# Seven products of halves for three experts: sums kept in PSUM, sums of weights and tokens placed by a table, a new order of all engines

## The chip, the cores and the metric

The kernel runs on one core of one Trainium2 chip. The metric is device time in microseconds (us), from runs of the whole kernel. The core has five engines that work side by side, each through its own queue in order: TensorE (PE in the rows, PEld for its weight loads), VectorE (DVE), ScalarE (ACT), GpSimd (POOL) and SyncE (SP), which here only issues transfers.

## The reference

Three layers follow one another. An mLSTM attention over 2 batches, 8 heads and 768 steps gives 1,536 tokens of 320 numbers. A dense layer with a rational function between its two products (320 to 2,048 to 320) follows. The last layer has four experts, whose outputs are added with a weight for each token:

```
def _moe2_ref(x, domain_probs, w1, w2):          # x (1536, 320), w1 (4, 320, 1024), w2 (4, 1024, 320)
    p = domain_probs / (domain_probs.sum(-1, keepdims=True) + 1e-09)
    out = np.zeros((N, D))
    for e in range(E):
        h = np.maximum(x @ w1[e], 0.0)
        out += p[:, e:e + 1] * (h @ w2[e])
    return out
```

The change is in experts 1 to 3 of this last layer, and in the order of the instructions from the dense layer on.

## The kernel before

**Numbers in two parts.** Every operand of a large product is held as a high part (fp32r) and a low part, the rest of the fp32 number. A product of a block is made of hi x hi, hi x lo, lo x hi, and for the last 64 of the 320 input rows (the "remainder") one matmul whose partitions hold these combinations side by side, 32 rows each.

**Seven products.** Experts 1 to 3 compute `x @ w1[e]` by Strassen's scheme in Winograd's form. The 320 inputs are cut in two (two blocks of 128 rows and a remainder of 2 x 32), the outputs of a block of 256 hidden units in two, and the tokens in two. A *stage* is one expert, one half `p` of the tokens (768) and one block `k` of 256 hidden units: 3 x 2 x 4 = 24 stages. A stage makes seven products of four matmuls of 384 columns (`product`, L1076), in three PSUM banks `ba`, `bb`, `bc` that come from a pool of two (`bank_new`), so that `bc` follows `ba` in its bank, the next stage's `ba` follows `bb`, and the next stage's `bb` follows `bc`. Products into a bank go on while VectorE takes partial sums out of it: `u2 = bb + s1` (L1154), `u3 = bb + s1` (L1162), `c21 = bb + s1` (L1173) and `c12 = bc + u2` (L1182), with `s1` a ScalarE copy of `ba`. `c22` is made by a ScalarE copy `s5` of `bc` (L1166) and a GpSimd sum `u3 + s5` (L1168). For each of the four blocks of the result ScalarE writes the relu as a high part (`relu`, L1096) and VectorE the low part (`low`, L1101). `low` reads `c` and the high part; for `c11` that is the bank `ba`, for `c21`, `c22`, `c12` a buffer in SBUF.

**Fills.** The second product (`g @ w2`) of a stage is 36 matmuls of 320 columns, which are laid between the products of the next stage, five or six at a time (`fill`, L1138). After the fourth `k` of a half, VectorE adds the six finished tiles to the output (`evac_exp`, L880), one in each fill.

**Preparation.** `prep(e, k)` loads a block of weights (9 transfers on SP), makes the sums of blocks that the scheme needs (4 of the main rows and 4 of the remainder, L1015) on GpSimd, lets ScalarE write the high parts (L1018, L1019, L1021), and subtracts for the low parts: main rows and second-layer weights on GpSimd (L1022, L1024), remainder rows on VectorE (L1023). `xprep(p)` does the like for a half of the tokens: sums on GpSimd and VectorE (L1040, L1046, L1057; L1057 writes three copies of each remainder half by three sums), low parts on both (L1050, L1064). Weights of expert 1 with `k` 0 and 1 and the tokens of half 0 go where the dense layer's weights were, those with `k` 2 and 3 where expert 0's weights are. The weights of the next expert are prepared during the four stages of the second half of the expert before. All temporary tiles come from five staging buffers (`stage`, L991).

**Order.** `ORDER` (L22) gives each engine a fixed order of its instructions, by their number in the order in which the program makes them. In the PE table, 2488 is the first matmul of stage 0; all before it in number belongs to earlier layers and expert 0. On VectorE the Strassen part begins with number 491, on ScalarE with 481, on GpSimd with 222, on SP with 95.

Of the kernel before, what the change touches and what calls it, by code (L numbers as in the profile page):

```python
# [92 lines left out]
    286-288 292-294 281 289 295 290 296-297 299 291 298 301-305 308 300 306 309-311 307 312-319 321-324 320 325-332  # L93
    334-338 343-344 333 345-348 340 339 349-350 341 351 342 352-357 361-362 358 363 359-360 364-366 368-370 367
    371-380 383-385 381 386-387 389 382 390 388 391-393 395-396 394 397-398 401 399 402 400 403-406 408-409 407 414
    410 415 411-412 416-417 413 418-423 425-429 424 430-434 436-441 435 442-445 448-449 447 450-453 446 454-458
    460-463 459 464 466-471 465 472-475 477-478 476 479-481 491 482 492 483 493 485 484 494 486 495-497 487 499-500
    488 498 501-503 489 504 490 519-521 505 522-527 506 528 507 529-533 508 534-535 509-510 536-537 511 513 538 514
    512 539-541 515 542-543 516-518 544-563 571 564-570 572-573 580 574-579 581-582 589 583-588 590-591 604 592-603
    605-643 651 644-650 652-653 660 654-659 661-662 669 663-668 670-671 684 672-683 685-754  # L100
# [15 lines left out]
    440-442 437 443 445-447 438 448-449 463 444 464 452-454 450 455 451 456 481-483 457 484-485 458 465-469 486 471  # L116
    470 487 472 474-475 488 473 490-491 476 489 492-494 477 495 478-480 511 496 512 497-498 513 499 514-517 500-501
    518-521 502 522-523 503 524-525 505-506 504 526-527 507-508 528-529 509-510 530-538 546 539 547 540-545 555-556
    549-550 548 551-554 564-565 558-559 557 560-563 573-574 567-568 566 569-572 575-598 606 599 607 600-605 615-616
    609-610 608 611-614 624-625 618-619 617 620-623 633-634 627-628 626 629-632 635-678  # L120
# [6 lines left out]
    133 143 132 150 144 148 153 149 151-152 136 145-146 154 157-158 155-156 160 159 167 222 161 223-225 162 226 228  # L127
    227 229 232 234 233 164 163 235-236 238 237 239 165-166 170 168-169 172 171 175 174 173 178 176-177 181 179-180
    182-188 190 189 191-192 194 193 195-196 198 197 200 199 202 201 204 203 206 205 208 207 210 209 212 211 214 213
    216 215 218 217 220 219 230 221 231 240 242 241 243-245 248 246 249 247 250-253 255 254 256-259 261 260 262 265  # L130
    267 266 269 268 270 263 288 264 271-273 275 274 276 289 277-278 281 279 282 280 283 290 284-286 294 287 295-298
# [1114 lines left out]
```

## Time and profile before

| | us |
|---|---|
| median of 3 runs | 689.5 (688.64 to 691.54) |
| the profiled execution, its own time | 691.14 |
| its span, first to last instruction | 689.3 |
| mean granted clock of TensorE | 0.97 of full speed |

| engine | busy us | share of the span |
|---|---|---|
| PE (matmul) | 623.3 | 90% |
| DVE | 497.0 | 72% |
| ACT | 370.5 | 54% |
| POOL | 372.0 | 54% |

The busy times are of the profiled execution. Busy time of PE contains matmuls that run at half clock, so a share of 90% is not the share of useful work.

### The profile page before, as it was taken

To read this page: it belongs to the slowest core of one execution; us is meant where nothing else is said; L and a number is where in the kernel's file an instruction comes from. 1 tells how busy PE (TensorE), PEld (TensorE's weight loads), DVE (VectorE), ACT (ScalarE), POOL (GpSimd) and SP (SyncE) were. 2 spreads that over 40 slices of the span, in tenths; PEclk is the share of its full clock that TensorE was granted. 3 is DMA by queue.
4 is the path that set the end of the run, shared out by engine and by line. 5 is a ranking of instruction groups with operands and counts; after the bars stand their busy time and mean duration, and the time that the engine had idled before them with its cause. 6 is when DMAs were issued, how large, how long until landed. Compare 5 with 4: busy or idle time off the path is not lost.

```text
span 689.3 us, 11395 instructions
## 1 busy us (share of the span) xinstructions
PE 623.3 (90%) x4300; PEld 601.9 (87%) x4300; DVE 497.0 (72%) x755; ACT 370.5 (54%) x682; POOL 372.0 (54%) x395
## 2 busy tenths in 40 slices
PE   3898999999999999999998866889869988899997
PEld 1888999999999999999997766889769988899997
DVE  8889999999887686676777678865764456643544
ACT  5989977576667557686873523334422244332221
POOL 6678897567774434353479867725841037421010
PEclk9889999999999999999999978999999999999999
DMA  7884431202200000000000200211210012000101
GB/s 209 256 250 134 123 118 57 84 24 77 88 20 0 2 0 1 1 2 1 2 20 11 63 19 16 57 36 48 56 48 1 1 34 54 24 1 0 58 1 58
DMA packets 21383, 35.46 MB, mean 51 GB/s; under 512 B 3377, under 2 KB 14129, under 8 KB 21329
## 3 DMA queue, kind: packets, MB, share of 16 engines
q1 hardware_dynamic: 21328, 34.74, 17.2%
q8 instruction: 34, 0.56, 0.4%
q14 instruction: 21, 0.16, 0.1%
...
## 4 chain that ended last, share of the span: by engine, by line
PE 55%; DVE 25%; ACT 6%; issue 5%; POOL 5%; DMA 2%; SPq 0%; ACTq 0%; POOLq 0%; DVEq 0%
PE h L1080 14%; PE acc L1114 14%; PE h L756 13%; PE acc L768 12%; DVE ar L1023 3%; DVE fb L637 2%; DVE ar L1101 2%; DMA so<-in_o_gate_dram 1%; DVE h L794 1%; DVE cv_t L379 1%; DMA qkt<-in_qk_dram 1%; ACT ar L1096 1%; DVE so L880 1%; POOL stg_r L1015 1%; POOL ar L1022 1%
## 5 line engine op out<-in xcount | busy, mean ns | idle before, releaser
L1080 PE MATMUL h<-ar,ar 128*128 128x384 f32 (+1 forms) x408 | 103.9, 353 | 29.4 <-DVE u L1154 13.0
L768 PE MATMUL acc<-wout,g 128*128 128x320 f32 x576 | 127.6, 320 | 1.7 <-POOL g L258 0.6
L756 PE MATMUL h<-x,win 128*128 128x256 f32 x768 | 126.5, 288 | 1.4 <-DVE s__2895 L795 0.7
L756 PEld LDWEIGHTS h<-x,win 128*128 128x128 f32 x768 | 107.8, 190 | 3.4 <-issue 0.9
L1080 PEld LDWEIGHTS h<-ar,ar 128*128 128x128 f32 (+1 forms) x408 | 73.2, 196 | 34.4 <-DVE u L1154 15.0
L1168 POOL TENSOR_TENSOR c<-u,s 128x384 f32<-128x384 f32 x24 | 24.3, 1013 | 134.6 <-ACT s L1166 134.6
L768 PEld LDWEIGHTS acc<-wout,g 128*128 128x128 f32 x576 | 93.1, 189 | 4.0 <-POOL g L258 1.1
L1114 PE MATMUL acc<-ar 128*128 128x320 f32 x432 | 81.8, 319 | 0.0
L1114 PE MATMUL acc<-ar,ar 128*128 128x320 f32 x432 | 80.0, 313 | 0.0
L1101 DVE SCALAR_TENSOR_TENSOR ar<-c,ar 128x384 fp32r<-128x384 f32 x72 | 57.6, 827 | 29.5 <-ACT ar L1096 29.4
L1096 ACT ACTIVATE ar<-c 128x384 fp32r<-128x384 f32 x72 | 35.9, 520 | 74.5 <-DVE c L1182 39.0
L1114 PEld LDWEIGHTS acc<-ar 128*128 128x128 f32 x432 | 73.0, 197 | 0.0
L756 PE MATMUL h<-x,we 128*128 128x256 f32 x384 | 71.4, 286 | 0.8 <-DVE g L805 0.8
L1114 PEld LDWEIGHTS acc<-ar,ar 128*128 128x128 f32 x432 | 71.1, 192 | 0.0
L768 PE MATMUL acc<-we,g 128*128 128x320 f32 x288 | 59.4, 320 | 4.9 <-ACT g L804 2.7
L756 PEld LDWEIGHTS h<-x,we 128*128 128x128 f32 x384 | 58.4, 192 | 1.6 <-DVE g L805 1.3
L1080 PE MATMUL h<-x,ar 128*128 128x384 f32 x216 | 51.4, 347 | 6.5 <-DVE c L1173 6.5
L1166 ACT ACTIVATE s<-h 128x384 f32<-128x384 f32 x24 | 11.8, 491 | 77.7 <-PE h L1080 77.7
L768 PEld LDWEIGHTS acc<-we,g 128*128 128x128 f32 x288 | 45.8, 193 | 6.9 <-ACT g L804 3.5
L1080 PEld LDWEIGHTS h<-x,ar 128*128 128x128 f32 x216 | 37.9, 195 | 7.2 <-DVE c L1173 6.8
L1173 DVE TENSOR_TENSOR c<-h,s 128x384 f32<-128x384 f32 x24 | 13.3, 556 | 38.3 <-PE h L1080 38.2
L1015 POOL TENSOR_TENSOR stg_m<-stg_m 128x128 f32<-128x128 f32 x48 | 28.4, 607 | 13.4 <-DMA stg_m<-in_moe_w_dram 13.4
...
## 6 DMA issues: line engine op xcount, KB each, us to landing
...
```

Of the source, the lines that this page charges most:

```text
L637: V.tensor_tensor_scan(W, src, id4f, 0.0, op0=ALU.mult, op1=ALU.add)
L756: PE.matmul(o, w5[:, j, fs], r, start=(n == 0), stop=(n == len(seq) - 1))
L768: PE.matmul(acc[t], x, y, start=(first and a == 0 and n == 0), stop=(last and a == nff - 1 and n == 2))
L1015: G.tensor_tensor(out=b[:, d], in0=b[:, x], in1=b[:, y], op=op)
L1023: V.tensor_tensor(out=wr[KR:2 * KR], in0=r7[KR:2 * KR], in1=wr[KR:2 * KR].bitcast(F32), op=ALU.subtract)
L1080: PE.matmul(bank, w, x, start=(first and n == 0), stop=(n == 3), skip_group_check=True)
L1096: A.activation(g[:, 0], c, AF.Relu)
L1101: V.scalar_tensor_tensor(out=g[:, 1], in0=c, scalar=0.0, in1=g[:, 0].bitcast(F32), op0=ALU.max, op1=ALU.subtract)
L1114: PE.matmul(acc[t], g[:, x, w * P:(w + 1) * P], wo[:, y, a], start=(k == 0 and a == 0 and n == 0), stop=(k == NK - 1 and a == 1 and n == 2))
L1166: A.activation(s5, bc, AF.Copy)
L1168: G.tensor_tensor(out=c22, in0=u3, in1=s5, op=ALU.add)
L1173: V.tensor_tensor(out=c21, in0=bb, in1=s1, op=ALU.add)
```

## The change

Four things change. **In the stage:** `c22` becomes one VectorE sum of the bank `bc` and `u3`, ScalarE applies the relu in place and writes the high part by a second instruction, and GpSimd writes the low part; `s5` goes. `c21` and `c12` are written back into their banks instead of into SBUF, and `relu` and `low` read them there. **In the preparation:** each sum and each low part goes to the engine that a string `ws` names. In the order in which it is read: `prep(1,0)` and `prep(1,1)` (11 instructions each) on VectorE, the 17 of `xprep(0)` on VectorE, `prep(1,2)` and `prep(1,3)` on GpSimd, of `xprep(1)` 15 on VectorE and its two main low parts on GpSimd, and all eight preparations for experts 2 and 3 on GpSimd. **In the remainder of the tokens:** one sum of 64 partitions is made, six SP transfers copy its halves to three places each, and seven copies with seven low parts become four and four. **In the order:** the tables are new from there to the end. The PE table lays numbers 2488 to 2502, the first 15 matmuls of stage 0, between the last matmuls of expert 0. The VectorE table swaps each `evac_exp` with the sum that follows it.

In the new numbering VectorE's Strassen part runs from 491: `prep(1,0)` 491-501, `prep(1,1)` 502-512, `xprep(0)` 513-529, `xprep(1)` 530-544, then 8 for each stage (`u2`, low of `c11`, `u3`, `c22`, `c21`, low of `c21`, `c12`, low of `c12`) and 6 more in each stage with `evac_exp`; stage 0 is 545-552, stage 4 is 577-590, stage 8 is 615-628. On GpSimd 222-243 are `prep(1,2)` and `prep(1,3)`, 244-245 the two of `xprep(1)`, then comes one low part of `c22` for each stage (246 for stage 0), and from stage 5 on the preparations. On ScalarE a stage is six numbers (505-510 for stage 0), and 540-542 is `prep(2,0)`. On SP the transfers of `xprep(0)` are 113-118 and those of `xprep(1)` 137-142.

```
--- before.py
+++ after.py
+    2298-2301 2305 2302-2304 2306-2316 2318-2335 2348-2351 2488-2489 2336-2337 2342-2343 2352-2353 2338-2341
+    2344-2347 2354-2363 2376-2382 2490 2492 2364-2365 2370-2371 2383-2384 2493-2494 2366-2369 2372-2375 2385-2391
+    2404-2410 2392-2393 2398-2399 2411-2412 2394-2397 2400-2403 2413-2419 2432-2438 2491 2420-2421 2426-2427
+    2439-2440 2496 2422-2425 2428-2431 2441-2447 2460-2466 2495 2448-2449 2454-2455 2467-2468 2450-2453 2456-2459
+    2469-2475 2497-2501 2476-2477 2482-2483 2502 2478-2481 2484-2487 2503-4023
...
+    472-475 477-478 476 479-481 499-501 482 510-511 513 483 512 514-516 485 484 517 519 518 521 520 486 522 487
+    523-524 526 525 527-528 488 529 489 545 490 546-549 551 550 552-560 530-531 561 532-533 562 534 563-564 535-536
+    565-568 537 569 541 538-539 570-571 540 542 572-576 543-544 578 577 580 579 582 581 584 583 586 585 587 589 588
+    590-614 616 615 618 617 620 619 622 621 624 623 625 627 626 628-652 654 653 656 655 658 657 660 659 662 661 663
...
+    467-469 471 470 487-488 472 474-475 473 489-492 476 505 477-478 506 479-480 493-494 507 509 508 510 495 511
+    496-497 512 498 513-518 499 519-520 500 521-523 501-502 524 503-504 525-533 540 534 541 535-539 549 543 542 544
...
+    201 204 203 206 205 208 207 210 209 212 211 214 213 216 215 218 217 220 219 221-222 224 223 225-226 228 227 229
+    233 235 234 236-237 239 238 240 230 246 231-232 241-242 247 243-244 248 245 252 254 253 255 249 256 258 257 259
+    264 266 265 267-268 270 269 271 250 260-261 276 251 277-279 272 262 273 263 280 282 281 284 274 283 288 290 289
+    285 291-292 275 293-296 286 297 304 306 305 307 287 308 310 309 316 311 317 298 318-320 299 321-323 300-302
...
+    103 93 95-96 106-109 97-102 104-105 110-162 169 163-168 170-180 187 181-186 188-198 205 199-204 206-207 214
+    208-213 215-226
...
+    ws="VVVVVVVVVVVVVVVVVVVVVVVVVVVVVVVVVVVVVVVGGGGGGGGGGGGGGGGGGGGGGVVVVVVGGVVVVVVVVVGGGGGGGGGGGGGGGGGGGGGGGGGGGGGGGGGGGGGGGGGGGGGGGGGGGGGGGGGGGGGGGGGGGGGGGGGGGGGGGGGGGGGGGG",
...
-            tr = [t[:, n] for n in range(7)]
+            tr = {B11: t[:, 0:1], B21: t[:, 1:3], T1: t[:, 3:5], T2: t[:, 5:7]}
         else:
             t = ar[1][0:96, o + 8 * HT:o + 11 * HT].rearrange("p (n t) -> p n t", n=3)
-            tr = [t[:, n] for n in range(3)]
-            for n in range(2):
-                t = g_p.tile([P, 1024], F32R, tag="g", name="xr")[0:96, 0:2 * HT].rearrange("p (n t) -> p n t", n=2)
-                tr += [t[:, 0], t[:, 1]]
+            tr = {B11: t[:, 0:1], B21: t[:, 1:3]}
+            for n in (T1, T2):
+                tr[n] = g_p.tile([P, 1024], F32R, tag="g", name="xr")[0:96, 0:2 * HT].rearrange("p (n t) -> p n t", n=2)
         xv.append((tm, tr))
...
-                    G.tensor_tensor(out=b[:, d], in0=b[:, x], in1=b[:, y], op=op)
+                    tt("ws", b[:, d], b[:, x], b[:, y], op)
...
-            G.tensor_tensor(out=wm[:, 1], in0=m7, in1=wm[:, 0].bitcast(F32), op=ALU.subtract)
-            V.tensor_tensor(out=wr[KR:2 * KR], in0=r7[KR:2 * KR], in1=wr[KR:2 * KR].bitcast(F32), op=ALU.subtract)
-            G.tensor_tensor(out=wo[:, 1], in0=w3, in1=wo[:, 0].bitcast(F32), op=ALU.subtract)
+            tt("ws", wm[:, 1], m7, wm[:, 0].bitcast(F32), ALU.subtract)
+            tt("ws", wr[KR:2 * KR], r7[KR:2 * KR], wr[KR:2 * KR].bitcast(F32), ALU.subtract)
+            tt("ws", wo[:, 1], w3, wo[:, 0].bitcast(F32), ALU.subtract)
...
-        def sums(r, np_, eng):
+        def sums(r, np_):
...
-                eng.tensor_tensor(out=o, in0=x0, in1=x1, op=op)
+                tt("ws", o, x0, x1, op)
             return ta, tb
 
         def main():
             r = [stage("xm")[:, 0:2 * HT] for j in range(2)]
-            for j, e in ((0, G), (1, V)):
-                e.tensor_tensor(out=r[j], in0=xj[0][j].bitcast(F32), in1=xj[1][j].bitcast(F32), op=ALU.add)
-            for n, t in enumerate(sums(r, P, G)):
+            for j in range(2):
+                tt("ws", r[j], xj[0][j].bitcast(F32), xj[1][j].bitcast(F32), ALU.add)
+            for n, t in enumerate(sums(r, P)):
                 hi, lo = tm[:, 0, 2 * n:2 * n + 2], tm[:, 1, 2 * n:2 * n + 2]
                 A.activation(hi, t, AF.Copy)
-                (V, G)[n].tensor_tensor(out=lo, in0=t, in1=hi.bitcast(F32), op=ALU.subtract)
+                tt("ws", lo, t, hi.bitcast(F32), ALU.subtract)
 
         def rem():
+            o = stage("xo")[:, 0:2 * HT]
+            tt("ws", o, xj[0][2].bitcast(F32), xj[1][2].bitcast(F32), ALU.add)
             r = [stage("xe")[0:96, 0:2 * HT] for j in range(2)]
             for j in range(2):
-                k = slice(j * KR, (j + 1) * KR)
                 for q in range(3):
-                    (G, V)[j].tensor_tensor(out=r[j][q * KR:(q + 1) * KR], in0=xj[0][2][k].bitcast(F32),
-                                            in1=xj[1][2][k].bitcast(F32), op=ALU.add)
-            ta, tb = sums(r, 96, G)
+                    SY.dma_start(out=r[j][q * KR:(q + 1) * KR], in_=o[j * KR:(j + 1) * KR])
+            ta, tb = sums(r, 96)
             r0, r1 = [t.rearrange("p (b t) -> p b t", b=2) for t in r]
-            for n, t in ((B11, r0[:, 0]), (B21, r1[:, 0]), (B22, r1[:, 1]), (T1, ta[:, 0]), (T3, ta[:, 1]),
-                         (T2, tb[:, 0]), (T4, tb[:, 1])):
-                A.activation(tr[n], t, AF.Copy)
-                V.tensor_tensor(out=tr[n][2 * KR:3 * KR], in0=t[2 * KR:3 * KR], in1=tr[n][2 * KR:3 * KR].bitcast(F32),
-                                op=ALU.subtract)
+            for n, t in ((B11, r0[:, 0:1]), (B21, r1), (T1, ta), (T2, tb)):
+                d = tr[n]
+                A.activation(d, t, AF.Copy)
+                tt("ws", d[2 * KR:3 * KR], t[2 * KR:3 * KR], d[2 * KR:3 * KR].bitcast(F32), ALU.subtract)
         return main, rem
 
...
-        return h, l, tr[n]
+        m = max(k for k in tr if k <= n)
+        return h, l, tr[m][:, n - m]
...
+        c22 = el_new("r", 2, "c22")
+        V.tensor_tensor(out=c22, in0=bc, in1=u3, op=ALU.add)
+        A.activation(c22, c22, AF.Relu)
+        g22 = g_new(1)
+        A.activation(g22[:, 0], c22, AF.Copy)
+        G.tensor_tensor(out=g22[:, 1], in0=c22, in1=g22[:, 0].bitcast(F32), op=ALU.subtract)
         product(bb, k, A22, p, T4, False)
-        s5 = el_new("x", 3, "s5")
-        A.activation(s5, bc, AF.Copy)
-        c22 = el_new("r", 2, "c22")
-        G.tensor_tensor(out=c22, in0=u3, in1=s5, op=ALU.add)
-        r22 = relu(c22, 1)
         fill(5)
         product(bc, k, S4, p, B22, False)
-        c21 = el_new("y", 4, "c21")
-        V.tensor_tensor(out=c21, in0=bb, in1=s1, op=ALU.add)
-        r21 = relu(c21, 0)
+        V.tensor_tensor(out=bb, in0=bb, in1=s1, op=ALU.add)
+        r21 = relu(bb, 0)
         g21 = low(r21)
-        g22 = low(r22)
         fill(6)
         q = (n - 1) % len(stages)
         if n and stages[q][1] == 1 and stages[q][0] < NE - 1:
             pre[stages[q][0] + 1, stages[q][2]][1]()
-        c12 = el_new("r", 2, "c12")
-        V.tensor_tensor(out=c12, in0=bc, in1=u2, op=ALU.add)
-        g12 = low(relu(c12, 1))
+        V.tensor_tensor(out=bc, in0=bc, in1=u2, op=ALU.add)
+        g12 = low(relu(bc, 1))
```

## Rows read from the trace of the kernel before

**Rows 1.** Windows from 350 us to PE's end: us, busy time by engine, PEclk, DMA.

```profile
350.00:390.20 40.20, 35.43 (x241) 33.56 (x240) 29.09 (x28) 19.10 (x35) 35.46 (x27) 0.96 0.13 37
390.20:447.10 56.90, 42.61 (x222) 39.98 (x221) 45.12 (x44) 20.79 (x40) 41.73 (x41) 0.85 0.11 30
447.10:523.30 76.20, 64.08 (x386) 62.64 (x385) 48.87 (x65) 26.73 (x48) 39.84 (x51) 0.98 0.15 42
523.30:553.90 30.60, 30.60 (x195) 30.60 (x194) 14.46 (x28) 9.14 (x19) 3.09 (x4) 1.00 0.00 1
553.90:606.95 53.05, 44.84 (x257) 43.79 (x256) 32.90 (x42) 19.36 (x35) 26.40 (x27) 0.94 0.14 37
606.95:685.50 78.55, 77.24 (x486) 76.45 (x484) 37.76 (x72) 21.36 (x45) 8.75 (x8) 1.00 0.06 21
```

**Rows 2.** Waits of PE from 380 us: us in total, times, longest.

```profile
PE h L1080 <- DVE u L1154: 13.0, 7, 3.0
PE h L1080 <- DVE c L1182: 12.3, 7, 3.2
PE h L1080 <- DVE c L1173: 6.5, 1, 6.5
```

**Rows 3.** Timeline of POOL, 393.7 to 402.2 us: start, us, line, shapes.

```profile
393.75 2.12 POOL L1022 TENSOR_TENSOR ar<-stg_m,ar 128x896 fp32r<-128x896 f32 x1
...
399.11 2.06 POOL L1022 TENSOR_TENSOR ar<-stg_m,ar 128x896 fp32r<-128x896 f32 x1
```

**Rows 4.** Timeline of DVE in the same stretch.

```profile
394.20 7.92 DVE L1023 TENSOR_TENSOR ar<-stg_r,ar 32x896 fp32r<-32x896 f32 x1
```

**Rows 5.** Instructions of L1101 (whole span) and L1023 (280 to 450 us): ns min/median/max.

```profile
L1101 DVE SCALAR_TENSOR_TENSOR ar<-c,ar x72: 545/559/3159, 403.3 to 681.3; 128x384 fp32r<-128x384 f32 x72
L1101 DVE SCALAR_TENSOR_TENSOR ar<-h,ar x24: 547/557/558, 393.2 to 674.2; 128x384 fp32r<-128x384 f32 x24
...
L1023 DVE TENSOR_TENSOR ar<-stg_r,ar x4: 1080/1712/7917, 353.6 to 407.8; 32x896 fp32r<-32x896 f32 x4
```

**Rows 6.** Groups of DVE and POOL, 447.1 to 685.5 us: busy us, mean ns.

```profile
L1023 DVE TENSOR_TENSOR ar<-stg_r,ar 32x896 fp32r<-32x896 f32 x8 | 17.4, 2177 | 0.2
...
L1168 POOL TENSOR_TENSOR c<-u,s 128x384 f32<-128x384 f32 x20 | 20.3, 1015 | 126.6 <-ACT s L1166 126.6
L1022 POOL TENSOR_TENSOR ar<-stg_m,ar 128x896 fp32r<-128x896 f32 x8 | 17.4, 2170 | 6.7 <-ACT ar L1018 6.7
L1015 POOL TENSOR_TENSOR stg_m<-stg_m 128x128 f32<-128x128 f32 x25 | 16.0, 651 | 11.6 <-DMA stg_m<-in_moe_w_dram 11.6
L1015 POOL TENSOR_TENSOR stg_r<-stg_r 96x128 f32<-96x128 f32 x28 | 13.7, 507 | 4.6 <-DMA stg_r<-in_moe_w_dram 4.4
L1024 POOL TENSOR_TENSOR ar<-stg_w,ar 128x640 fp32r<-128x640 f32 x8 | 12.8, 1600 | 3.5 <-ACT ar L1021 3.1 <-PE h L1080 0.4
```

**Rows 7.** Timeline of PE over the end of one undisturbed stage.

```profile
637.52 1.04 PE L1114 MATMUL acc<-ar 128*128 128x320 f32 x6
638.40 0.69 PE L1080 MATMUL h<-x,ar 128*128 128x384 f32 x3
...
639.84 0.69 PE L1080 MATMUL h<-ar,ar 128*128 128x384 f32 x3
```

**Rows 8.** Timeline of DVE in the same stage.

```profile
636.29 0.56 DVE L1173 TENSOR_TENSOR c<-h,s 128x384 f32<-128x384 f32 x1 [2.31 <-PE h L1080]
637.55 1.03 DVE L1101 SCALAR_TENSOR_TENSOR ar<-c,ar 128x384 fp32r<-128x384 f32 x2 [0.71 <-ACT ar L1096]
```

**Rows 9.** Timeline of ACT in the same stage.

```profile
639.16 0.53 ACT L1096 ACTIVATE ar<-c 128x384 fp32r<-128x384 f32 x1 [1.65 <-DVE c L1182]
```

**Rows 10.** Timeline of DVE near 345 us: L794 writes PSUM, L795 SBUF.

```profile
344.55 0.69 DVE L794 SCALAR_TENSOR_TENSOR h<-s__4022,h 128x512 f32<-128x512 f32 x1
345.27 0.69 DVE L795 SCALAR_TENSOR_TENSOR s__4022<-h,r__4024 128x512 f32<-128x512 f32 x1
```

**Rows 11.** Transfers that SP issues at the end: ns min/median/max.

```profile
L882 SPq DMA_DIRECT2D out_dram<-so x6: 332/332/345, 682.4 to 686.1; - x6
```

More of the change, by code (lines that the diff above doesn't have):

```diff
@@ L92 @@
     267-268 237 269 234 270-271 224-225 272 275-276 273 277 274 235 278 239 279 240 280 246-248 282-285 249 238
[L93 to L100, printed above, removed]
+    286-288 292-294 281 289 295 290 296-297 299 291 298 301-305 308 300 306 309-311 491 307 492-494 312-316 495
+    317-319 321-324 320 325-332 334-338 343-344 333 496-497 345-348 340 339 349-350 341 498 502 351 342 352-354
+    503-504 355-357 361-362 358 363 359-360 364-366 505-506 508 507 509 368-370 367 371-380 383-385 381 386-387 389
+    382 390 388 391-393 395-396 394 397-398 401 399 402 400 403-406 408-409 407 414 410 415 411-412 416-417 413
+    418-423 425-429 424 430-434 436-441 435 442-445 448-449 447 450-453 446 454-458 460-463 459 464 466-471 465
+    472-475 477-478 476 479-481 499-501 482 510-511 513 483 512 514-516 485 484 517 519 518 521 520 486 522 487
+    523-524 526 525 527-528 488 529 489 545 490 546-549 551 550 552-560 530-531 561 532-533 562 534 563-564 535-536
+    565-568 537 569 541 538-539 570-571 540 542 572-576 543-544 578 577 580 579 582 581 584 583 586 585 587 589 588
+    590-614 616 615 618 617 620 619 622 621 624 623 625 627 626 628-652 654 653 656 655 658 657 660 659 662 661 663
+    665 664 666-690 692 691 694 693 696 695 698 697 700 699 701 703 702 704-728 730 729 732 731 734 733 736 735 738
+    737 739 741 740 742-772
     """,
@@ L115 @@
     399 409-410 405 416-417 413 418 411 414 419 415 420 422-424 412 425-427 421 428-429 432-434 430 435-436 439 431
[L116 to L120, printed above, removed]
+    440-442 437 443 445-447 438 448-449 463 444 464 452-454 450 455 451 456 481-483 457 484-485 458 465-466 486
+    467-469 471 470 487-488 472 474-475 473 489-492 476 505 477-478 506 479-480 493-494 507 509 508 510 495 511
+    496-497 512 498 513-518 499 519-520 500 521-523 501-502 524 503-504 525-533 540 534 541 535-539 549 543 542 544
+    550 545-548 558 552 551 553-554 559 555-557 567 561 560 562 568 563-566 570 569 571-593 600 594 601 595-599 609
+    603 602 604 610 605-608 618 612 611 613-614 619 615-617 627 621 620 622-623 628 624-626 630 629 631-672
     """,
@@ L126 @@
     82 125 124 81 86 122 129 101 87-88 126-127 134 89 130 128 102-103 94 137 131 104 140 135 138 142 139 147 117 141
[L127 to L131, printed above, removed]
[L132 to L135 removed]
+    133 143 132 150 144 148 153 149 151-152 136 145-146 154 157-158 155-156 160 159 167 161-162 164 163 165-166 170
+    168-169 172 171 175 174 173 178 176-177 181 179-180 182-188 190 189 191-192 194 193 195-196 198 197 200 199 202
+    201 204 203 206 205 208 207 210 209 212 211 214 213 216 215 218 217 220 219 221-222 224 223 225-226 228 227 229
+    233 235 234 236-237 239 238 240 230 246 231-232 241-242 247 243-244 248 245 252 254 253 255 249 256 258 257 259
+    264 266 265 267-268 270 269 271 250 260-261 276 251 277-279 272 262 273 263 280 282 281 284 274 283 288 290 289
+    285 291-292 275 293-296 286 297 304 306 305 307 287 308 310 309 316 311 317 298 318-320 299 321-323 300-302
+    312-313 328 303 329-331 324 314 325 315 332 334 333 336 326 335 340 342 341 337 343 327 344 346 345 348 338 347
+    349 339 350-357
     """,
```

9 lines of the change are left out of this document (removed).

## Prediction

> **What bounds the kernel now.** I read the page first (PE 90% busy, DVE and POOL far less), then windows from 350 us on, then the waits of PE, then the timelines of DVE and POOL around the longest waits. The windows show where time is lost [rows 1]. From 523.3 to 553.9 us three stages take 30.60 us and PE is busy all of it: a stage without a wait is 10.2 us. Its 36 fills take 0.147 us each (six between 637.52 and 638.40 [rows 7]), 5.3 us together, so the 28 matmuls of the products are 4.9 us. Against this measure:
>
> - 390.2 to 447.1, stages 0 to 3: 56.9 us; stage 0 has no fills, so 4.9 + 3 x 10.2 = 35.5 are needed: 21.4 lost.
> - 447.1 to 523.3, stages 4 to 9: 76.2 - 61.2 = 15.0 lost.
> - 523.3 to 553.9: nothing.
> - 553.9 to 606.95, stages 13 to 16: 53.05 - 40.8 = 12.25 lost.
> - 606.95 to 685.5, stages 17 to 23 and the last 36 fills: 78.55 - 71.4 - 5.3 = 1.85 lost.
> - 350 to 390.2, the end of expert 0: 40.2 - 35.43 = 4.8 idle, and a granted clock of 0.96 for another 1.6: 6.4 lost.
>
> That is 50.5 us in the stages and 6.4 ahead of them; idle time is not all of it, since at clocks of 0.85 and 0.94 matmuls after a wait run partly at the lower level. Every large wait of PE is for DVE: `u2`, `c12`, `c21` [rows 2]. These sums are short; what is late is the DVE queue ahead of them. At 394.20 one subtraction of the weights (L1023) took 7.92 us [rows 4], where four such took 1.08 at least [rows 5]. It ended 0.95 us after a run of POOL instructions that lasted from 393.75 to 399.11 + 2.06 = 401.17 [rows 3]. The eight later ones took 2.18 on average [rows 6]. `low` shows which operands matter: from a bank (`h`) it took 547 to 558 ns in 24 cases, from SBUF 545 to 3159 in 72 [rows 5]. So a DVE instruction whose two tensors both lie in SBUF waits for POOL; one with an operand in PSUM does not. The chain is PE, behind DVE, behind POOL.
>
> The Trainium skill (SBUF — State Buffer, section "Who interferes with whom") states the same split, one SBUF input against two, and adds that the loser waits for the whole instruction of the other. The 7.92 us of the trace are longer than any one POOL instruction, so here the measurement goes further than the page. By the page alone the wait at 394.20 would have ended with the POOL instruction then running, at 393.75 + 2.12, some 5 us sooner; by the page, then, rival 1 below has no such form, and the trace of this kernel shows that it has.
>
> **Stages 5 to 23.** Before, a stage has eight DVE instructions, three of which read SBUF twice (low of `c21`, `c22`, `c12`), and L1023 comes once for each of eight preparations. After, it has eight as well: `c22` comes, its low part goes to POOL, and all others have one operand in PSUM. L1023 goes to POOL. So no DVE instruction of these stages meets POOL any more, and of the 15.0 + 12.25 + 1.85 = 29.1 us (nothing in stage 4) nearly all should go. A write into PSUM costs DVE no more: 0.69 beside 0.69 [rows 10]. ScalarE gives up `s5` and gains a copy: one for one.
>
> Two things are new. First, POOL. A preparation cost it 4 x 0.65 + 4 x 0.51 + 2.17 + 1.60 = 8.4 us, and a stage 1.0 for `c22` [rows 6]. Now L1023 is added; POOL's price for 32 partitions is not shown, and lies between DVE's 1.08 [rows 5] and the 2.17 of 128 partitions; I take 2.2, since 96 partitions of L1015 cost nearly as much as 128. The low part of `c22` costs the 1.0 of the sum it replaces. That is 11.6 us for a stage of 10.2 in four stages running: 5.6 us late at their end. Weights of `k` are free after stage `k` of the second half and wanted four stages later, some 30 us of room, and `g22` is first read at the 22nd of the next stage's 36 fills. POOL stays off the path; if this room were gone, each expert would wait 5.6.
>
> Second, the banks are held longer. The next stage's `ba` waits for the low part of `c21`, its `bb` for that of `c12`, where before both waited only for the sum. In the undisturbed stage `c21` begins at 636.29 and takes 0.56, the relu 0.53 [rows 9], the low part 0.56: with three hand-overs of 0.05 to 0.1 it is done by 638.1, and `ba` is wanted at 638.40 [rows 7, 8]. For `c12` the relu also waits until the fills have read the buffer that it overwrites, at 637.52 + 1.04 = 638.56; then 0.53 + 0.56 and three hand-overs, 639.8 to 639.95, where `bb` is wanted at 639.84. So this chain just fits, or is 0.1 us late in each stage: 19 x 0.05 = 1. The ScalarE table lays a high part of weights ahead of this relu (540 ahead of 534), in the time in which the relu waits anyway; I add 1 us for eight such stages. The swaps with `evac_exp` take away the 0.6 that these cost before.
>
> With 1 more for what I don't see, 3 of 29.1 are left: **-26**. Ends: all goes (-29), or the bank chain is 0.5 late in 19 stages, 9.5, and 3 stay (-17).
>
> **Stages 0 to 4.** 15 of the 28 matmuls of stage 0 now run ahead of it (2.6 us of work). Weights `k` 0 and 1 and tokens 0 are done on DVE ahead of stage 0; `k` 2 and 3 on POOL in stages 0 and 1, 2 x (2.2 + 2.2 + 1.6) = 12 us, which ends about when stage 2 wants them. What stays is `xprep(1)`: 15 DVE instructions that read SBUF twice, spread by the table over the end of stage 1 to the beginning of stage 4 (530 to 544), while POOL works on `k` 3 and on sums for expert 2. Uncontended, by 1.08 us for 896 columns [rows 5], some 14 x 0.6 to 1.0 = 11 us in three stages, where DVE has 8 x 0.56 = 4.5 of its own in 10.2: it fits. With POOL each can wait 0.5 (a sum) to 2.1 (a low part); I take 0.7 on average, 10 us, of which half falls into DVE's free time. So I expect 5 us of waits, 2 of lower clock behind them, and 3 at the start of stage 0, where no fills cover the sums: 10.5 left of 21.4, **-11**. The last two low parts (543, 544) come behind the low part of `c12` of stage 3, and stage 4's second product needs the last of them at once: 1.5 to 3 of the 5. Ends: 4.5 left (-17); as much lost as before (0).
>
> The six transfers for each half are issued by SP at 0.33 each [rows 11], 2 us, and loads are queued behind them. For tokens 0, two sums with the results of expert 0 behind them wait on DVE until they have landed; an estimate from the last output (issued at 686.1, over at the span's end, 689.3) is 3 us each. The table puts other work between; if this cover fails, it costs 3 us.
>
> **Ahead of stage 0.** The 15 matmuls and a DVE without POOL beside it fill about half of the 6.4 lost: **-3** (0 to -5). The 16 sums of weights that move to DVE earlier, in the dense layer, cost it some 0.3 each by the same 1.08, and POOL is relieved of as many: 0, plus or minus 1.5.
>
> **Sum.** -26 - 11 - 3 = -40 from 691.14, the profiled execution's own time, gives 651. The median of the runs is 1.6 below that execution; I take 650 for the median after.
>
> **Rivals.**
> 1. *DVE starves at the front.* If `xprep(1)` meets POOL as L1023 did at 394.20, one such case costs 7, and stages 0 to 4 lose the 21 of before: 650 + 11 = 661. For it: 15 instructions, and POOL busy there. Against: POOL's runs are then of shorter instructions for the most part, 0.5 to 0.65 for a sum [rows 6].
> 2. *The bank chain is the new bound.* At 0.5 us late in each of 23 stages: 650 + 11 = 661. For it: no slack at 639.84. Against: the hand-overs in the rows are under 0.1.
> 3. *POOL falls behind* with the weights of experts 2 and 3, at stages 8 and 16: 2 x 8 = 16, so 666. It needs POOL at 1.7 times its rows: 4 x (19.7 - 10.2) = 38, 8 more than the room of 30.
> 4. *Waits only move*: the same loss in other places, 690.
> 5. *Slower:* the bank chain again, with the relu of `c12` stuck behind other ScalarE work (high parts of weights, copies). It decides from 40 / 23 = 1.75 us a stage; at 2.2 it would give 700. Such work would have to come first in each stage, and only eight stages have high parts of weights.
>
> **How the numbers follow.** My forecast, 640 to 660, has 0.58; rival 1 0.18; rival 2 0.14; rival 3 0.04; rival 4 0.03; rival 5 0.03. The range runs from 638 (all ends good but a little) to 667 (rivals 1 to 3 in). 0.5%, 3.4 us, is about what a measurement can tell from no change: faster 0.94, same 0.03, slower 0.03.
>
> **What would show it.** Right: `low` at 0.55 us throughout, PE without waits from stage 5 on and stages of 10.2 to 10.3 us, PE's waits all in stages 0 to 4, clock 1.00 after. Wrong: waits of `product` for the low part in every stage (rival 2), DVE instructions of `xprep` over 2 us (rival 1), waits for POOL's low parts of weights (rival 3).

## The result, and the profile after

The median fell from 689.07 us (4 runs, 688.63 to 691.54) to 639.14 us (4 runs, 637.76 to 646.54): ratio 0.929, 95% interval 0.9216 to 0.9365. 650 was forecast, with a range of 638 to 667. The profiled executions are 691.14 and 639.66, so -51.5 is to be explained.

The head of the page of the kernel after: busy time, share and count of each engine, and the clock by slices.

```profile
PE 609.8 (96%) x4300; PEld 592.6 (93%) x4300; DVE 450.5 (71%) x773; ACT 372.2 (58%) x676; POOL 334.2 (52%) x361
...
PEclk9879999999999999999999999999999999999999
```

PE went from 90% to 96% of a shorter span, and the granted clock is at 0.9 or more from the fourth of the 40 slices on. The waits of PE from 380 us, the view of [rows 2]:

```profile
PE h L1084 <- DVE ar L1105: 1.2, 1, 1.2
PE h L1084 <- DVE xr L263: 1.1, 1, 1.1
PE acc L773 <- DVE g L810: 0.2, 1, 0.2
```

The long waits for `u2`, `c12` and `c21` are gone. Windows, the view of [rows 1], cut where PE ends a stage: from the end of expert 0, stages 0 to 4, 5 to 10, 11 to 13, 14 to 18, 19 to 23:

```profile
351.50:388.95 37.45, 35.72 (x254) 34.26 (x253) 27.93 (x38) 19.24 (x33) 10.21 (x18) 1.00 0.22 59
388.95:435.46 46.51, 44.20 (x270) 42.81 (x270) 32.16 (x57) 23.54 (x41) 26.90 (x29) 1.00 0.19 47
435.46:497.00 61.54, 61.54 (x388) 61.43 (x387) 29.70 (x55) 26.69 (x48) 43.20 (x51) 1.00 0.19 52
497.00:527.30 30.30, 30.30 (x192) 30.27 (x191) 15.98 (x30) 11.39 (x22) 8.71 (x9) 1.00 0.07 20
527.30:578.34 51.04, 51.04 (x321) 50.96 (x321) 24.76 (x46) 21.81 (x40) 29.24 (x28) 1.00 0.10 27
578.34:634.50 56.16, 56.16 (x357) 55.94 (x355) 27.97 (x52) 15.58 (x31) 5.08 (x5) 1.00 0.08 29
```

From stage 5 on elapsed time and PE's busy time are the same number in every row, although POOL is busier than before in the stages that prepare weights (43.20 of 61.54 in stages 5 to 10, against 39.84 of 76.20 in stages 4 to 9 [rows 1]). `low`, which took up to 3159 ns before [rows 5]:

```profile
L1105 DVE SCALAR_TENSOR_TENSOR ar<-h,ar x72: 539/557/560, 387.3 to 629.8; 128x384 fp32r<-128x384 f32 x72
```

### The profile page after: what moved, and what is told of

The parts are those of the page before. It is cut to its first block, busy times and chain, and to the rows that moved or that the text cites. A ratio compares the mean times of both kernels' runs of the same rounds, so it can differ in the third digit from the quotient of the medians.

```text
span 637.8 us, 11387 instructions
## 1 busy us (share of the span) xinstructions
PE 609.8 (96%) x4300; PEld 592.6 (93%) x4300; DVE 450.5 (71%) x773; ACT 372.2 (58%) x676; POOL 334.2 (52%) x361
## 4 chain that ended last, share of the span: by engine, by line
PE 69%; DVE 20%; ACT 6%; issue 2%; POOL 1%; DMA 1%; SPq 0%; ACTq 0%; POOLq 0%; DVEq 0%
PE acc L1118 19%; PE h L1084 17%; PE h L761 15%; PE acc L773 13%; DVE fb L642 2%; DVE ar L263 1%; DVE h L799 1%; PE sc L669 1%; DVE cv_t L384 1%; PE o L694 1%; DVE g L810 1%; DVE x L742 1%; DVE qc L650 1%; DVE fb L674 1%; PE dl L709 1%
## 5 line engine op out<-in xcount | busy, mean ns | idle before, releaser
L1084 PE MATMUL h<-ar,ar 128*128 128x384 f32 (+1 forms) x408 | 99.4, 338 | 0.0
L1118 PE MATMUL acc<-ar 128*128 128x320 f32 x432 | 78.6, 309 | 0.0
L1100 ACT ACTIVATE ar<-h 128x384 fp32r<-128x384 f32 x72 | 35.3, 491 | 73.7 <-PE h L1084 46.8
L1105 DVE SCALAR_TENSOR_TENSOR ar<-h,ar 128x384 fp32r<-128x384 f32 x72 | 40.0, 556 | 48.0 <-ACT ar L1100 47.1
L1173 POOL TENSOR_TENSOR ar<-c,ar 128x384 fp32r<-128x384 f32 x24 | 24.4, 1016 | 93.7 <-ACT ar L1172 88.8
L1084 PEld LDWEIGHTS h<-ar,ar 128*128 128x128 f32 (+1 forms) x408 | 70.4, 188 | 0.8 <-DVE u L1166 0.3
L1118 PEld LDWEIGHTS acc<-ar 128*128 128x128 f32 x432 | 69.6, 188 | 0.0
L1170 ACT ACTIVATE c<-c 128x384 f32<-128x384 f32 x24 | 12.6, 526 | 60.3 <-DVE c L1169 60.3
L263 POOL TENSOR_TENSOR stg_m<-stg_m 128x128 f32<-128x128 f32 x40 | 19.5, 507 | 40.1 <-DMA stg_m<-in_moe_w_dram 24.1
L1158 DVE TENSOR_TENSOR u<-h,s 128x384 f32<-128x384 f32 x24 | 13.3, 556 | 24.6 <-PE h L1084 24.6
```

Of the source, the lines that this page charges most:

```text
L263: return ENG[alt(kind)].tensor_tensor(out=out, in0=in0, in1=in1, op=op)
L1084: PE.matmul(bank, w, x, start=(first and n == 0), stop=(n == 3), skip_group_check=True)
L1100: A.activation(g[:, 0], c, AF.Relu)
L1105: V.scalar_tensor_tensor(out=g[:, 1], in0=c, scalar=0.0, in1=g[:, 0].bitcast(F32), op0=ALU.max, op1=ALU.subtract)
L1118: PE.matmul(acc[t], g[:, x, w * P:(w + 1) * P], wo[:, y, a], start=(k == 0 and a == 0 and n == 0), stop=(k == NK - 1 and a == 1 and n == 2))
L1158: V.tensor_tensor(out=u2, in0=bb, in1=s1, op=ALU.add)
```

## The experiments

Theory P is that of the prediction: a VectorE instruction with two operands in SBUF waits for GpSimd's reads, and TensorE waits behind VectorE. Theory Q is that the new tables and the different load of VectorE made the gain, theory B that sums in place hold the banks too long. The table gives, beside the medians, the distance between the starts of `u2` (read from VectorE's timeline) of stages 0 and 5, and of stages 5 and 23; at 10.18 a stage, 18 stages are 183.2. Two things are to be kept in mind. The `u2` of stage 0 runs among the last matmuls of expert 0 where 15 matmuls of stage 0 are moved there, so the column 0 to 5 of f1 can't be set against that of after. And in the kernel before the first wait of stage 5 lies ahead of its `u2`, so 2.6 us that stages 5 to 23 lose stand in the column 0 to 5.

| kernel | median us | u2 of 0 to 5 | u2 of 5 to 23 |
|---|---|---|---|
| before | 689.07 | 70.98 | 209.42 |
| b1, before, GpSimd only writes | 668.14 | 68.71 | 186.54 |
| b3, before, remainder low parts on GpSimd | 681.13 | 72.80 | 200.49 |
| b4, b3 and sums in place | 687.49 | 66.06 | 207.63 |
| after | 639.14 | 54.20 | 183.61 |
| a1, after, sums in SBUF | 648.63 | 58.39 | 189.10 |
| a2, after, remainder low parts on VectorE | 657.70 | 55.37 | 201.63 |
| a3, a1 and a2 | 668.90 | 59.43 | 207.97 |
| a4, after, c22 as before | 662.86 | 65.75 | 195.28 |
| f1, after, early matmuls moved back | 642.39 | 50.72 | 183.86 |
| f2, after, evac_exp not swapped | 647.17 | 55.84 | 190.08 |
| f4, after, GpSimd reads during xprep(1) | 644.20 | 58.89 | 183.91 |

Medians of the kernel before, in the groups of runs beside these: 690.74 (b3, b4, f4), 690.87 (a4, f1, f2), 691.50 (b1, a1 to a3). They lie 1.7 to 2.4 us above the 689.07 beside after, and after was not run again in these groups, so a difference of medians to 639.14 is uncertain by about as much. The traces allow a second count, from the start of the 2,529th matmul, which in all of these kernels is the same point ahead of stage 0 (350.2 us before, 351.6 after), to the end. By it a1, a2, a3, a4, f1, f2 and f4 are 9.4, 18.9, 29.3, 22.9, 3.6, 7.8 and 4.7 us longer than after, and b1, b3 and b4 are 25.5, 7.4 and 7.1 shorter than before.

**Do GpSimd's reads cause the loss?** b1 changes GpSimd alone:

```
-    G.tensor_tensor(out=b[:, d], in0=b[:, x], in1=b[:, y], op=op)
+    G.memset(b[:, d], 0.0)                     # experts 2 and 3; likewise for L1022 and L1024
```

> The kernel before, in which GpSimd's sums and low parts of the weights of experts 2 and 3 are replaced by fills with zero of the same tiles (same count and order on every engine, but GpSimd reads nothing there); the weights of experts 2 and 3 are therefore not the reference's, and GpSimd's instructions may also be shorter. VectorE's work, order and operands are as before. Theory P: L1023 falls from 2.2 to about 1.1 us and the low parts to 0.55 us throughout, and the 12 to 29 us lost in stages 5 to 23 go: 660 to 675 against 689. Theory Q (the length and order of VectorE's queue): within 3 us of before, 686 to 692.

668.14 against 691.50, ratio 0.9668 (0.9599 to 0.9737). Groups of b1 from 447.1 us on, columns as in [rows 6]:

```profile
L1110 DVE SCALAR_TENSOR_TENSOR ar<-c,ar 128x384 fp32r<-128x384 f32 x63 | 33.3, 556 | 27.3 <-ACT ar L1105 27.3
...
L1029 DVE TENSOR_TENSOR ar<-stg_r,ar 32x896 fp32r<-32x896 f32 x8 | 8.7, 1081 | 0.3
...
L1026 POOL MEMSET ar<- 128x896 f32 x8 | 6.8, 852 | 4.8 <-PE h L1089 4.5
```

The subtraction fell from 2177 [rows 6] to 1081 ns and `low` to 556, with VectorE's queue as it was. In the last column, 25.8 us lie between before and after; 22.9 of them are gone here. But GpSimd's instructions are shorter here too (852 ns against 2170), so b1 alone does not separate reading from load. The next kernel does.

**The port by itself.** "The port" stands here for whatever VectorE and GpSimd have to share if theory P holds. m1 runs VectorE beside an idle GpSimd, beside six sums of 128x896 back to back, or beside one such sum with 21 sums of 128x128 or eight fills behind it. It was executed once and computes nothing of the reference.

```
    V.tensor_tensor(out=x[32:64], in0=a[32:64, 0:896], in1=x[32:64], op=ALU.subtract)     # L69, x2
    V.tensor_tensor(out=x[:, 0:384], in0=a[:, 0:384], in1=x[:, 0:384], op=ALU.add)        # L74, x4
    V.tensor_tensor(out=x[:, 0:384], in0=bank[:, 0:384], in1=x[:, 0:384], op=ALU.add)     # L79, x4
```

> The port by itself, in a kernel that computes nothing of the reference: VectorE runs two 32x896 subtractions (both operands in SBUF), four 128x384 sums (both in SBUF), or four of them with one operand in PSUM, beside a GpSimd that is idle, runs six 128x896 sums back to back, runs 22 short sums of 128x128, or only writes zeros. If VectorE waits for a whole run of GpSimd instructions: one VectorE instruction beside the six long ones takes as long as what is left of them, 7 to 12 us, and the next is undisturbed. If it waits for the one then running: each takes 1 to 3 us beside the long ones and 0.6 to 1.2 beside the short ones. Beside writes alone, and with one operand in PSUM: as beside an idle GpSimd, 1.08 and 0.55.

VectorE's timeline, in order: beside an idle GpSimd (9.69, 17.96, 26.38), the long sums (34.79, 51.45, 67.42), the short ones (82.63, 96.30), the fills (109.53, 121.20):

```profile
9.69 2.20 DVE L69 TENSOR_TENSOR x<-a,x 32x896 f32<-32x896 f32 x2
...
17.96 2.33 DVE L74 TENSOR_TENSOR x<-a,x 128x384 f32<-128x384 f32 x4
...
26.38 2.33 DVE L79 TENSOR_TENSOR x<-bank,x 128x384 f32<-128x384 f32 x4
...
34.79 5.01 DVE L69 TENSOR_TENSOR x<-a,x 32x896 f32<-32x896 f32 x2
...
51.45 8.63 DVE L74 TENSOR_TENSOR x<-a,x 128x384 f32<-128x384 f32 x4
...
67.42 2.33 DVE L79 TENSOR_TENSOR x<-bank,x 128x384 f32<-128x384 f32 x4
...
82.63 2.60 DVE L69 TENSOR_TENSOR x<-a,x 32x896 f32<-32x896 f32 x2
...
96.30 2.99 DVE L74 TENSOR_TENSOR x<-a,x 128x384 f32<-128x384 f32 x4
...
109.53 2.20 DVE L69 TENSOR_TENSOR x<-a,x 32x896 f32<-32x896 f32 x2
...
121.20 2.34 DVE L74 TENSOR_TENSOR x<-a,x 128x384 f32<-128x384 f32 x4
```

A sum of two SBUF operands goes from 0.58 to 2.16 us beside the long sums; with one operand in PSUM, or beside fills that keep GpSimd as busy, nothing changes. In this run of equal sums it waits for one GpSimd instruction at a time, not for the run: 2.5 us for each 32x896, where the rest of the run was over 10.

That left the 7.92 us of [rows 4] open. m2 lets GpSimd write different tiles, so that its instructions do not depend on each other, or runs a mixed row like that of the kernel before; it too was executed once and computes nothing of the reference.

```
+        for o in many:
+            G.tensor_tensor(out=o, in0=go, in1=b[:, 0:896], op=ALU.add)
```

> What the first measurement of the port left open, the 7.92 us that one VectorE instruction took in the kernel before while GpSimd ran five instructions in a row; the kernel computes nothing of the reference. GpSimd's run is now a chain (each instruction reads what the one before it wrote), or six to seven instructions that write different tiles, or a mixed run of such instructions like that of the kernel before; VectorE has one or two 32x896 subtractions or four 128x384 sums beside it. Theory 1: instructions of GpSimd that do not depend on each other follow without a gap, and VectorE gets the port only when the run ends: 6 to 13 us for the first VectorE instruction beside such a run, 2.5 beside the chain. Theory 2: the port changes hands after each instruction in every case: 1 to 3 us for each, and the 7.92 us have another cause.

Beside six independent sums:

```profile
33.34 4.89 DVE L73 TENSOR_TENSOR x<-a,x 32x896 f32<-32x896 f32 x2
...
51.66 2.09 DVE L77 TENSOR_TENSOR lo<-x,lo 32x896 fp32r<-32x896 f32 x1
```

2.1 to 2.5 each again. Beside the mixed row the means are 1.1 to 1.7, but they hide one long wait: of four sums that take 0.56 each undisturbed, one took 3.13 us. It began at 111.89 and ended behind GpSimd's last sum, so it had stood through that one and a short one as a whole. VectorE, then GpSimd beside it:

```profile
L82 DVE TENSOR_TENSOR x<-a,x x4: 557/1164/3129, 109.5 to 115.1; 128x384 f32<-128x384 f32 x4
```
```profile
111.40 1.17 POOL L64 TENSOR_TENSOR many<-go,b 96x128 f32<-96x128 f32 x2
112.54 2.07 POOL L65 TENSOR_TENSOR pool<-go,b 128x896 f32<-128x896 f32 x1
```

The full kernels show the same, and more of it. In b1 and b3, which up to there run as the kernel before, the 7.92 us come back as 8.01 and 8.05, each beside the same row of six GpSimd instructions. In a1 a low part took 4.50 us beside three of 2.13, 1.56 and 0.44, and a3 has three such of 4.5. VectorE in b3, VectorE in a1, and GpSimd in a1:

```profile
394.68 8.05 DVE L1020 TENSOR_TENSOR ar<-stg_r,ar 32x896 fp32r<-32x896 f32 x1
```
```profile
459.73 4.50 DVE L1105 SCALAR_TENSOR_TENSOR ar<-c,ar 128x384 fp32r<-128x384 f32 x1 [0.65 <-PE h L1084]
```
```profile
459.74 2.13 POOL L263 TENSOR_TENSOR ar<-stg_m,ar 128x896 fp32r<-128x896 f32 x1
461.84 1.56 POOL L263 TENSOR_TENSOR ar<-stg_w,ar 128x640 fp32r<-128x640 f32 x1
463.37 0.44 POOL L263 TENSOR_TENSOR stg_r<-stg_r 96x128 f32<-96x128 f32 x1
```

So neither theory holds in every case. Beside equal sums VectorE came in after the one then running, and beside mixed rows it sometimes stood through two to five whole ones. What decides which of the two happens stays open.

**Undoing one part of after.** a1 takes the sums out of the banks:

```
-        V.tensor_tensor(out=bb, in0=bb, in1=s1, op=ALU.add)
+        c21 = el_new("y", 4, "c21")
+        V.tensor_tensor(out=c21, in0=bb, in1=s1, op=ALU.add)
...
+        c12 = el_new("r", 2, "c12")
+        V.tensor_tensor(out=c12, in0=bc, in1=u2, op=ALU.add)
```

> The kernel after, with the sums c21 and c12 written to SBUF buffers again (as in the kernel before) and everything else, the tables too, as after. The two low parts of a stage then read SBUF twice. Theory P (a VectorE instruction with two SBUF operands waits for GpSimd's reads of SBUF, and in-place sums are what frees it): the low parts of c21 and c12 stretch from 0.55 us to 1 to 3 us in the stages in which GpSimd prepares weights (5 to 8 and 13 to 16), stages 5 to 23 lose 5 to 12 us again, so 644 to 651 against 639. Theory Q (the new tables and the shorter VectorE queue made the gain, the place of the sums does not matter): under 1 us, 638 to 640. Theory B (the banks are held longer by sums in place, which costs something): 1 to 2 us faster than after.

648.63, 9.5 more; 5.5 of it lies in stages 5 to 23, as P said, and 4.2 in stages 0 to 4, of which it said nothing. The group of low parts from 430 to 680 us, and the largest wait of PE:

```profile
L1105 DVE SCALAR_TENSOR_TENSOR ar<-c,ar 128x384 fp32r<-128x384 f32 x40 | 46.0, 1151 | 19.1 <-ACT ar L1100 15.6 <-PE h L1084 3.3
```
```profile
PE h L1084 <- DVE u L1158: 6.3, 5, 1.4
```

1151 ns against 557, and `u2` late behind them: P. The stages without preparation stay at 10.18, so the banks cost after nothing there: B falls. a2 puts the eight subtractions back:

```
-            tt("ws", wr[KR:2 * KR], ...)     # "G" for experts 2 and 3
+            tt("ws", wr[KR:2 * KR], ...)     # "V"; in VectorE's table ahead of u2 of stages 5 to 8 and 13 to 16
```

> The kernel after, with the low parts of the remainder weights of experts 2 and 3 (eight instructions of 32x896) on VectorE again instead of GpSimd, each ahead of u2 of its stage, ScalarE's order moved in three places for it. By their shortest time, 1.08 us, they fit into a stage, in which VectorE is busy for 4.5 of 10.2 us. Theory P: each of the eight waits for GpSimd's running instructions, 2 us or more on average with single ones of 4 to 8, and the sums behind them are late: 8 to 14 us lost in stages 5 to 8 and 13 to 16, so 647 to 653. Theory Q (load alone counts): 1.08 each, mostly covered, 0 to 2 us, 639 to 641.

657.70, 18.6 more, beyond P's end. The eight, with what VectorE's idle time ahead of them ended on:

```profile
L262 DVE TENSOR_TENSOR ar<-stg_r,ar x8: 1080/1722/2568, 440.6 to 571.4; 32x896 fp32r<-32x896 f32 x8
its engine sat idle before it (us, times) until:
  ACT ar L1022: 12.6, 7
  DMA stg_r<-in_moe_w_dram: 4.3, 1
```

Their mean is 1.82 us (14.5 / 8), only 5.9 us over eight of 1.08. More, 16.9 us, was VectorE standing still in front of them, for a high part or a load not yet there, with `u2` queued behind. So P has the sign but not the size: my place in the queue made most of it. a3 joins both edits.

> Both edits together: c21 and c12 in SBUF, and the remainder low parts of experts 2 and 3 on VectorE; the sum c22 stays with VectorE and its low part with GpSimd. Theory P: the sum of the two single losses or more, 15 to 28 us, most of the 29 that stages 5 to 23 lost before, so 654 to 667. Theory Q: 0 to 2 us, 639 to 641.

668.90: 29.8 more, against 9.5 + 18.6 for the two alone. That is the sum or a little more, as P said, and 2 us beyond its end; but the eight stand at the same place in the queue as in a2. The clean measure of the move is b3, on the kernel before:

```
-            V.tensor_tensor(out=wr[KR:2 * KR], ...)
+            (G if e > 1 else V).tensor_tensor(out=wr[KR:2 * KR], ...)
```

> The kernel before, with the low parts of the remainder weights of experts 2 and 3 (eight instructions) on GpSimd instead of VectorE, and nothing else. Theory P: they leave VectorE's path, the eight waits of 2.2 us and what they make late go; the low parts of c21, c22 and c12 still read SBUF twice. About 12 us faster, 675 to 681 against 689. Theory Q (new tables made the gain): within 3 us of before; GpSimd has 2.2 us more in eight stages, so it may even be slower.

681.13, ratio 0.9834 (0.9779 to 0.9889): 9.6 less by the medians and 7.4 by the traces. That is far from Q and most of P's 12, though just outside its 675 to 681.

**The bank chain.** b4 adds the sums in place to b3, still in the old order, with `c22` on GpSimd and its low part on VectorE:

> The kernel before, with the same eight low parts on GpSimd and with c21 and c12 written in place in PSUM; the tables, the evac_exp order, the c22 sum on GpSimd with its low part on VectorE, the token preparation and everything up to stage 4 stay as before. Theory P: these two edits are most of the gain of stages 5 to 23; only the low part of c22 still reads SBUF twice there: 22 to 28 us faster, 661 to 667. Theory Q: within 3 us of before.

687.49 (10 runs, 683.81 to 694.91), ratio 0.9942 (0.99 to 0.9983). The time is near Q's, the reason is not: in the traces it is, against b3, 6.7 shorter up to stage 5 and 7.1 longer from there to 23. All of PE's waits in the Strassen part are now for low parts:

```profile
PE h L1078 <- DVE ar L1099: 28.2, 32, 3.2
```

So in place alone gives back later what it frees at the front: the next stage's bank hangs on the low part, and other work stands ahead of it. a4 takes the `c22` edit out of after to see whether that work is `c22`'s low part:

```
-        V.tensor_tensor(out=c22, in0=bc, in1=u3, op=ALU.add)
-        A.activation(c22, c22, AF.Relu)
...
+        A.activation(s5, bc, AF.Copy)
+        G.tensor_tensor(out=c22, in0=u3, in1=s5, op=ALU.add)
+        r22 = relu(c22, 1)
...
         g21 = low(r21)
+        g22 = low(r22)
```

> The kernel after, with c22 made as in the kernel before (ScalarE copy of the bank, sum on GpSimd, relu to the high part, low part on VectorE between the low part of c21 and the sum c12); c21 and c12 stay in place, the tables stay except for this place. Theory C (the c22 edit is what makes the bank chain fit): in the undisturbed stages of b4_rem_pool_sums_inplace this low part takes 0.47 us of VectorE between c21 and c12 and the next stage's second product starts 0.2 us late; that is 20 x 0.2 = 4 us, and in the eight stages in which GpSimd prepares weights it meets GpSimd's reads and is 0.5 to 1 us longer, 4 to 8 us: 647 to 651 against 639. Theory P alone (one more instruction with two SBUF operands in eight stages, chain has room): 4 us at most, 640 to 643, and no wait in stages without preparation.

662.86: 23.7 more, far beyond both. VectorE and TensorE of a4 in an undisturbed stage:

```profile
510.61 0.56 DVE L1104 SCALAR_TENSOR_TENSOR ar<-h,ar 128x384 fp32r<-128x384 f32 x1 [0.61 <-ACT ar L1099]
511.08 0.55 DVE L1104 SCALAR_TENSOR_TENSOR ar<-c,ar 128x384 fp32r<-128x384 f32 x1
511.55 0.56 DVE L1183 TENSOR_TENSOR h<-h,u 128x384 f32<-128x384 f32 x1
512.74 0.56 DVE L1104 SCALAR_TENSOR_TENSOR ar<-h,ar 128x384 fp32r<-128x384 f32 x1 [0.64 <-ACT ar L1099]
```
```profile
513.35 0.96 PE L1083 MATMUL h<-ar,ar 128*128 128x384 f32 x4 [0.21 <-DVE ar L1104]
```

and of after in such a stage:

```profile
505.75 0.56 DVE L1105 SCALAR_TENSOR_TENSOR ar<-h,ar 128x384 fp32r<-128x384 f32 x1 [0.56 <-ACT ar L1100]
506.23 0.56 DVE L1184 TENSOR_TENSOR h<-h,u 128x384 f32<-128x384 f32 x1
507.43 0.56 DVE L1105 SCALAR_TENSOR_TENSOR ar<-h,ar 128x384 fp32r<-128x384 f32 x1 [0.64 <-ACT ar L1100]
```
```profile
508.18 0.69 PE L1084 MATMUL h<-ar,ar 128*128 128x384 f32 x3
```

In after the last low part ends at 507.99 and the bank is wanted at 508.18: 0.19 of room. The low part of `c22` (511.08) takes 0.47 in that chain, and a stage goes from 10.18 to 10.66 to 10.73 us. That I expected 0.2 from b4's wait was wrong: the idle time shown is not the whole delay, since the first product behind it takes 0.96 instead of 0.86, and fills end later too. So stages 5 to 23 lose 11.7, half a microsecond and a little more in each. Stages 0 to 4 lose 11.6 more in the table, and that is not this chain alone: there the low part of `c22` meets GpSimd's reads and takes up to 2.00 us. What each share of the 11.6 is was not taken apart.

f2 undoes the swaps:

```
-    ... 578 577 580 579 582 581 584 583 586 585 587 589 588 590-614 ...
+    577-772
```

> The kernel after, with each evac_exp of VectorE ahead of the sum that follows it again, as in the kernel before. Theory: since the sums in place release the banks only with their low parts, a sum that is 0.55 us later makes the next stage's products later by nearly as much, in five stages with evac_exp: 2 to 4 us, 641 to 643. Rival: TensorE's fills cover it, 0 to 0.5 us.

647.17: 8.0 more, twice the end of what I expected. Each stage with `evac_exp` takes 11.31 to 11.37 and the one ahead of it 10.72 to 10.75 us, 1.1 and 0.55 over 10.2: about 1.65, five times. In b1, too, the stages ahead of an `evac_exp` (7, 11, 15, 19) took 10.65 to 10.73: 2.0 of the 2.9 us that b1 leaves, so this loss was in the kernel before.

**The front.** f4 has GpSimd read SBUF while VectorE prepares the second half of the tokens:

```
+    for _ in range(4):
+        G.tensor_tensor(out=dum, in0=dum, in1=dum, op=ALU.subtract)
```

> The kernel after, with four more subtractions of 128x768 on GpSimd (about 2 us each by the 2.1 us of 128x896, operands in SBUF, in a tile that nothing else uses) placed where GpSimd stood idle in the trace of after, 404 to 412 us, just when VectorE prepares the second half of the tokens. Theory: the front gained 10 us more than forecast because GpSimd happened to be idle there. Then VectorE's instructions of the token preparation stretch to 2 us and more each, and 3 to 9 us are lost in stages 1 to 4: 642 to 648 against 639. Rival (the front gained by placement on VectorE and the new table alone): GpSimd's work is off the path, 0 to 1 us.

644.20: 5.1 more, 4.7 of it between the `u2` of stages 0 and 5. VectorE in f4, then GpSimd in f4:

```profile
404.25 3.15 DVE L262 TENSOR_TENSOR xm<-x 128x768 f32<-128x768 f32 x2
...
407.79 3.09 DVE L262 TENSOR_TENSOR xt<-xm 128x384 f32<-128x384 f32 x2
```
```profile
404.40 7.80 POOL L1142 TENSOR_TENSOR dum<-dum 128x768 f32<-128x768 f32 x4
```

and the same in after, where GpSimd stood idle around its two low parts:

```profile
404.07 1.89 DVE L263 TENSOR_TENSOR xm<-x 128x768 f32<-128x768 f32 x2
...
406.35 1.01 DVE L263 TENSOR_TENSOR xt<-xm 128x384 f32<-128x384 f32 x2
```
```profile
408.32 1.85 POOL L263 TENSOR_TENSOR ar<-xt,ar 128x768 fp32r<-128x768 f32 x1 [4.05 <-ACT ar L1053]
...
420.26 2.10 POOL L263 TENSOR_TENSOR stg_m<-stg_m 128x128 f32<-128x128 f32 x4 [6.12 <-DMA stg_r<-in_moe_w_dram]
```

f1 puts the 15 early matmuls back:

```
-    ... 2488-2489 2336-2337 ... 2490 2492 ... 2497-2501 2476-2477 2482-2483 2502 2478-2481 2484-2487 2503-4023
+    ... 2484-4023
```

> The kernel after, with the first 15 matmuls of stage 0 behind the last matmul of expert 0 again (and the VectorE and ScalarE instructions that follow them moved back with them). If the table of TensorE filled idle time ahead of stage 0: 2 to 3 us lost, all before 392 us, 641 to 642 against 639. If the waits at the end of expert 0 are only moved into stage 0: within 0.5.

642.39, 3.3 more by the medians. In the traces it is 3.6, of which 3.4 are there by the `u2` of stage 1: the early matmuls fill time that is idle otherwise.

## Why the prediction was right, and where its size was off

By the profiled executions the terms are these.

- **Stages 5 to 23:** forecast -26, ends -29 and -17; measured -29.1, all that was lost. The cause was as told: in the column 5 to 23, b1 takes 22.9 of 25.8 away from the kernel before, b3 alone 8.9, and a1 brings 5.5 back. "This chain just fits" held, with 0.19 us of room; the 3 us kept for it and for the unseen were not needed. What the step did not see is how much hangs on it: I priced `c22` as "one for one" on ScalarE, and a4 shows that it is worth 11.7 us here (23.7 in all), because without it the chain doesn't fit. GpSimd's subtraction of 32x896, taken as 2.2 us, took 2.12. Rival 2 is thus real in b4 and a4, but not in this change.
- **Stages 0 to 4:** forecast -11, ends -17 and 0; this is the term that was mis-sized. 46.51 us for 13 matmuls of stage 0 (2.3) and four stages (40.8) is 3.4 lost of 21.4: -18.0. The 15 instructions took 10.6 us in all, as their uncontended price said (11). The step that failed is "I take 0.7 on average, 10 us, of which half falls into DVE's free time": none was held by GpSimd by more than 0.1 us, since it stood idle 4.05 and 6.12 us around its two low parts. With the 2 us of lower clock and most of the 3 at the start of stage 0 also absent, that is the 7 us. (The three parts of what was to be left, 5, 2 and 3, add up to 10 and not 10.5.) f4 prices what was missing: with four sums on GpSimd at that place they lose 4.7, close to the 5 forecast. That GpSimd would be idle just then, waiting for ScalarE and for transfers, the prediction did not foresee, so as much of this term is luck. Of what was named, stage 4's wait for the last low part is there with 1.1 (forecast 1.5 to 3), and one of 1.2 at the start of stage 1.
- **Ahead of stage 0:** forecast -3, ends 0 and -5. The stretch from 351.5 began at 350.2 before. 37.45 us for the 33.6 of work that it held then (40.0 less 6.4 lost) and 2.6 moved into it: 1.2 lost, so -5.2. f1 confirms the matmuls' part with 3.3 to 3.6.
- **Dense layer:** 0 plus or minus 1.5; by the same two starts, +1.3.

The sum is -29.1 - 18.0 - 5.2 + 1.3 = -51.0, of -51.5. What was to show it did: `low` at 0.55 us throughout, stages of 10.2, full clock, all waits ahead of stage 5.

Rival 1 did not come, because its condition did not: none of the 15 instructions was held by GpSimd. Its price of 7 us for a case is not refuted. The 7.92 us came back as 8.01 in b1 and 8.05 in b3, and TensorE's wait for the `c21` behind it, 6.5 us [rows 2], is 6.6 in b3. By the rule of the Trainium skill (SBUF — State Buffer, section "Who interferes with whom") the loser waits for the whole instruction of the other. The 2.1 to 2.5 us beside instructions of 2.1 to 2.2 in m1 and m2 agree with it; the 8 us of before, b1 and b3, the 4.50 of a1 and the 3.13 of m2, each past several instructions, go beyond it, as the prediction said of the first.

The -18.0 of stages 0 to 4 was not undone move by move, so how it is shared among the engines chosen in `ws`, the copies by transfers and the new order stays open. What the order tables give beyond the edits that were undone one by one was not tried, nor was a version with 544 ahead of 543, which could take away at most the 1.1 us of stage 4's wait.
